# Where a query transpose starts, which buffer the extra keys leave through, and which of two transposes goes first

## The chip, the cores and the metric

The kernel runs on one core of one Trainium2 chip. The metric is the device time in microseconds (us) of one execution; lower is better. The core has a matrix engine (TensorE, PE in the profile), a vector engine (DVE), a scalar engine (ACT), GpSimd (POOL) and a queue engine (SP) that here does nothing but issue transfers. Each engine runs its own instruction stream in order, and engines wait for one another on semaphores.

## The reference

There are two parts. The first is a recurrent attention with memory over 2048 rows of width 640, in 64 segments of 32 rows, with 32 heads of width 128. The 8 memory rows of a segment are outputs of the segment before, so the segments follow one another strictly:

```
mem = mem0
for s in range(64):
    h = concat([mem, layernorm(x)[32*s : 32*s+32]])        # 8 + 32 rows
    q, k, v = h @ Wq, h @ Wk, h @ Wv                       # 640 -> 32 heads x 128
    p = softmax(where(mask, q @ k.T * scale, -1e9))        # memory rows see all, others causally
    o = (p @ v) @ Wo
    mem, out[s] = o[:8], o[8:]
h  = x + out
h2 = h + ((relu(layernorm(h) @ W_gate)) * (layernorm(h) @ W_up)) @ W_down
```

The second part, the last two lines, is a feed-forward block over all rows.

## The kernel before, in words

**The order is written by hand.** The function `add` records operations with the keys that they read and write; `solve` then derives the semaphore waits from these keys: an operation waits for the last writer of what it reads, and for all readers of what it overwrites. Each engine runs its operations in the order in which they were recorded. So a key in a list of reads is also a way to hold an operation back, and a buffer that a transfer still reads holds back whoever wants to fill it again.

**Steps.** The loop over `s` (L905) handles one segment per step. A step projects 32 rows through Wk, Wq and Wv: 8 memory rows, which are known only at the end of the step before, and 24 "rider" rows of later segments, whose normed values are known long in advance. A step therefore computes keys, queries and values that a later step needs. Since 24 riders per step are fewer than the 32 rows that a segment has, 32 more rows per four steps ("extra" rows, in `act_e`) are projected in gaps: in a step with s % 4 = 2 through Wk, with 3 through Wq, with 0 through Wv (`extra_units`, L858). The step with s % 4 = 1 fills the same gaps with the output projection of older rows (`woe_pass`). In what follows a step is called by its class, s % 4.

**Order inside a step.** TensorE: K projection (`project`, L422 and L400), Q projection, two fifths of V, `pick_mem` (L453, picks the memory queries), the rest of V, `scores` (L572), two gap pieces, `pv_mem` (L609), gap pieces, `trans_om` (L624), the last gap piece, `wo_pass` (L644, the new memory rows), `pv_x` (L690). Then the next step's K projection starts.

**Token buffers.** A projection leaves PSUM as rows (tokens) in `tok[0..3]`, copied by ACT and DVE (`to_tok`, which shows as L464 on ACT and L466 on DVE). K's rows go to `tok[0]` and `tok[1]`, which together are `tokp[0]`; Q's rows go to `tok[2]` and `tok[3]`, together `tokp[1]`. A DMA transpose from SP (`dma_t`, L363) turns `tokp[0]` into `KS`, and another, `trans_q`, turns `tokp[1]` into `QS`. From `KS`, DVE copies the riders' keys to the ring `Kr` (`evac_k`); from `QS`, ACT copies the riders' queries to the ring `Qr` (`evac_q`). `scores` of a step reads this step's own `KS` for the memory keys, and `Kr` and `Qr` as earlier steps left them. A third transpose per step, `trans_ox`, turns `ox` into `oT`.

**The place of `trans_q`.** In classes 0 and 1 (`qlate`) it stands at the end of the step and its copy goes into the next step through `late_k`. In classes 2 and 3 it stands early:

```
            qlate = nr and s % 4 < 2
            if nr and not qlate and s < NSEG - 2:
                trans_q()
            loads()
```

and its copy by ACT follows `exp_x` and `v_riders` in the same step.

**The extra keys** of class 2 are copied by ACT to `tok[2]` and `tok[3]` after the last gap piece and then transposed from `tokp[1]` straight to `Kr`. **The normed rows**: once per four steps, in class 2, DVE scales the rows `xt` of the next block (`row_scale`, L383), SP transposes them into `at`, and in the next step POOL copies them into the activations (`ln1_back`, L524). In four steps of class 0 (s = 32, 36, 40, 44) the same pair of operations handles rows of the feed-forward part. The transpose `at<-xt` is recorded after `pv_x`.

**Riders' values** go from `Vp` to the ring `Vr` by DMAs from POOL (`v_riders`, L501): eight in class 2, four in the others. Output rows leave by `attn_d<-wtok` and `attn_d<-at`, also from POOL.

**Probabilities of the memory queries**: `exp_mem` has ACT compute the exponentials into `om` (L582), and two DVE operations write them, masked, into `Pbd` (L585).

Of the kernel before, what the change touches and what calls it, by code (L numbers as in the profile page):

```python
# [208 lines left out]
def build_kernel(nc, A_x, A_mem0, A_Wq, A_Wk, A_Wv, A_Wo, A_seg_len, B_W_gate, B_W_up, B_W_down, out):  # L209
    _, S, D = A_x.shape  # L210
    M = A_mem0.shape[1]
# [4 lines left out]
    NSEG = S // SEG  # L216
# [145 lines left out]
    def dma_t(dst, src, r, w):  # L362
        add("sp", lambda e: e.dma_start_transpose(dst, src), r=r, w=w, dma=True)  # L363
# [65 lines left out]
    def to_tok(b, t, eng):  # L429
        copy_op(eng, tok[t][:, :], bank(b), [B(b)], [("tok", t)])  # L430
# [150 lines left out]
    def exp_mem():  # L581
        add("act", lambda a: a.activation(ap(om, 0, [[8, 2], [16, 8], [1, 8]]), s_view(0, M), ACTF.Exp,  # L582
                                          scale=SCALE), r=[B(P0), B(P1)], w=[("om",)])
        for i in range(2):
            add("dve", lambda v, i=i: v.tensor_tensor(ap(Pbd, 256 * i, [[32, 8], [16, 2], [1, 16]]),  # L585
                                                      ap(om, 0, [[16, 8], [0, 2], [1, 16]]),
                                                      ap(mbd, 32 * i, [[0, 8], [16, 2], [1, 16]]), ALU.min),
                r=[("om",), ("mbd",)], w=[("Pbd", i)])

    def exp_x():  # L590
        add("act", lambda a: a.activation(ap(Px, 0, [[32, 2], [64, 8], [1, 32]]), s_view(M, M + SEG),  # L591
# [266 lines left out]
    def extra_units(s):  # L858

        b, r = (s - 2) // 4, (s - 2) % 4
        t0 = 64 + 128 * b + 96
        if b < 0 or r == 3 or t0 >= S:
            return None, None, None
        a, ks = act_e[b % 2], [("acte", b % 2)]
        q = seg_slot(t0 // SEG)
        j = (1, 0, 2)[r]

        def part(n):
            project(a, ks, j, (0, 1), BQ, PARTS[n], j // 2)

        def evac():
            for i, e in enumerate(("act", "act")):
                if j == 2:
                    to_v(BQ[i], Vr[q], i, ("Vr", q), e)
                else:
                    to_tok(BQ[i], 2 + i, e)
            if j == 1:  # L880
                dma_t(Kr[q][:].rearrange("p h t -> p (h t)").rearrange("p (k r) -> p k r", r=128), tokp[1][:, :],
                      [("tok", 2), ("tok", 3)], [("Kr", q)])

        def fin():
            trans_q()
            late_q.append(lambda: evac_q(QS, ("QS",), t0, 32, 0, "act"))
        return part, evac, (fin if j == 0 else None)
# [17 lines left out]
    for s in range(NSEG):  # L905
        last = s == NSEG - 1
        q = seg_slot(s)
        nb = s // 4 + 1
        ln = 64 + 128 * nb < S

        e2 = EARLY.index(s // 4 * 4 + 3) if s // 4 * 4 + 3 in EARLY else None
        e2b = EARLY.index(s - 1) if s - 1 in EARLY else None
        def loads(s=s, e2=e2, e2b=e2b, nb=nb, ln=ln):
            if s % 4 == 3 and e2 is not None:
                dma(xt[:, :], x_ap[128 * e2:128 * e2 + 128, :], r=[("KS",)], w=[("xt",)])
                load_attn(at, e2, [], ("at",))
            if s % 4 == 0 and ln and e2b is None:
                ln1_load(nb, xt, ("xt",))
            if s % 4 == 1 and s - 2 in EARLY:
                e = EARLY.index(s - 2)  # L920
                dma(xn2_d[e], at[:, :], r=[("at",)], w=[("xn2_d", e)])
                if ln:
                    ln1_load(nb, xt, ("xt",))
        if s == 0:
            loads()
        if s > 0:
            a, ks, kn = pass_act(s)
            t0, nr = rider_tokens(s)
            project(a, ks, 1, (0, 1), BQ, (0, 1), spare=16)
            ks = ks + kn  # L930
            project(a, ks, 1, (0, 1), BQ, (2, 3, 4), spare=24)
            to_tok(BQ[0], 0, "act")
            to_tok(BQ[1], 1, "dve")
            if last:
                break
            dma_t(KS[:].rearrange("p h t -> p (h t)").rearrange("p (k r) -> p k r", r=128), tokp[0][:, :],
                  [("tok", 0), ("tok", 1)], [("KS",)])
            trans_ox()
            for f in late:
                f()  # L940
            late = []
            project(a, ks, 0, (0, 1), (P0, P1), spare=40)
            to_tok(P0, 2, "act")
            to_tok(P1, 3, "dve")
            for f in late_k + late_q:
                f()
            late_k, late_q = [], []
            qlate = nr and s % 4 < 2
            if nr and not qlate and s < NSEG - 2:
                trans_q()  # L950
            loads()
            project(a, ks, 2, (0, 1), (P2, P3), (0, 1), spare=16)
            if s == NSEG - 2:
                trans8(tok[2], ("tok", 2), tok[3], ("tok", 3), T0)
                copy_op("dve", Qr[:, :, q, 0:M], slots(T0, 0, M), [B(T0)], [("Qm", q)])
                evac_q(slots(T0, 0, SEG), B(T0), t0, nr, M, "act")
            else:
                pick_mem(T0)
                copy_op("dve", Qr[:, :, q, 0:M], bank(T0)[:, 0:256].rearrange("p (h t) -> p h t", t=M), [B(T0)], [("Qm", q)])
            if nr:  # L960
                evac_k(KS, ("KS",), t0, nr, M, "dve")
            project(a, ks, 2, (0, 1), (P2, P3), (2, 3, 4), spare=24)
            to_v(P3, Vp, 1, ("Vp", 3), "dve")
            to_v(P2, Vp, 0, ("Vp", 0), "act", 0, 2)
            scores(s)
            exp_mem()
            to_v(P2, Vp, 0, ("Vp", 1), "act", 2, 4)
            exp_x()
            if nr:
                v_riders(t0, nr)  # L970
                if s < NSEG - 2 and not qlate:
                    evac_q(QS, ("QS",), t0, nr, M, "act")
        units, evac, nfin = extra_units(s)
        woe = s % 4 == 1 and s >= 5

        def filler(n):
            if units:
                units(n)
            if woe:
                woe_pass(BQ[0], WPARTS[n])  # L980
        filler(0)
        filler(1)
        pv_mem(s)
        if s % 4 == 1 and s >= 5:
            copy_op("dve", oTn[:, :, :], oT[:, :, 0:M], [("oT", "m"), ("oT", "n")], [("oTn",)])
        elif s > 0:
            copy_oTe(s - 1)
        norm_om()
        filler(2)
        filler(3)  # L990
        trans_om(128 if s % 4 < 2 else 32)
        mask_x()
        n = n_rows(nb) if s % 4 == 2 and ln else 128 if e2b is not None else 0
        if n:
            row_scale(xt, ("xt",), n, xt, ("xt",))
        filler(4)
        if evac:
            evac()
        if woe:
            copy_op("dve", oTe[:, :, 0:M], oTn[:, :, :], [("oTn",)], [("oTe", 0)])  # L1000
            woe_sum(BQ[0])
            late.append(lambda b=s // 4 - 1: woe_store(b, [("KS",)]))
        if s == 0:
            wo_pass(T1, None, halves=(0,))
            keep_busy(P0)
            wo_pass(T1, None, halves=(1,))
        else:
            wo_pass(T1, MARKS[s % 4])
        if s == NSEG - 2:
            load_gate_up([("oTe", (s - 1) % 4), ("go", T1, 0)])  # L1010
        to_act(s + 1, B(T1), bank(T1)[:, 0:160])
        if s >= 1:
            wo_rows(T1, wtok[s % 2], ("wtok", s % 2), "act")
            store_attn(wtok[s % 2], ("wtok", s % 2), s - 1)
            if qlate and s < NSEG - 2:
                trans_q([("act", (s + 1) // 4 % 2, (s + 1) % 4, "m")])
                late_k.append(lambda t0=t0, nr=nr: evac_q(QS, ("QS",), t0, nr, M, "act"))
        pv_x(s, P0)
        if n:
            dma_t(chunks_of(at[:, :])[:, :, 0:n], xt[0:n, :], [("xt",)], [("at",)])  # L1020
            if s % 4 == 2:
                late.append(lambda nb=nb: ln1_back(nb, chunks_of(at[:, :]), [("at",)], "pool"))
        if nfin:
            nfin()
        norm_x(P0)
        if s % 4 == 1 and ln:
            late.append(lambda nb=nb: row_stats(xt, ("xt",), n_rows(nb)))
        if s % 4 == 3 and e2 is not None:
            def f(e2=e2):
                add_attn(xt[:, :], xt, at, [("xt",), ("at",)], [("xt",)])  # L1030
                dma(h_d[128 * e2:128 * e2 + 128, :], xt[:, :], r=[("xt",)], w=[("h_d", e2)])
                row_moments(xt, ("xt",), 128)
            late.append(f)
            late_q.append(lambda: row_rstd(128))
# [218 lines left out]
```

## Time and profile before

| what | value |
|---|---|
| three runs, median (lowest to highest) | 1100.82 us (1099.63 to 1101.9) |
| the profiled execution, its own time | 1100.57 us |
| its span, first to last instruction | 1098.8 us |
| time around the span | 1.8 us |
| TensorE busy in the span | 1057.8 us (96%) |
| DVE, ACT, POOL busy | 608.4, 362.6, 291.5 us |
| steps 2 to 62, mean length | 13.55 us |
| `QS`, `KS`, `oT` transposes | 76, 62, 62 |
| `Kr<-tok` and `at<-xt` transposes | 15 and 19 |

A line of the groups names the line of the code, the engine, the operation, what it writes and reads, and how often; after the bar come its busy time, the mean duration of one in ns, and the idle time of the engine before it with what ended it. In the view of DMA issues the last number is the median time in us from issue to landing. In a timeline the first column is the start in us from the start of the span, the second the length, and brackets hold the idle time before and what ended it; "SPq" is SP's queue, where a length is the time that issuing took, not the transfer.

A step is measured here from the first matmul of `pv_x` of the step before to that of its own, so times "in the step" count from there.

### The profile page before, as it was taken

How to read it: one execution, taken by the hardware profiler on the slowest of the kernel's cores; microseconds unless marked ns; L12 is line 12 of the kernel's file. 1: busy time of each engine (PE TensorE's matmuls, PEld its weight loads, DVE VectorE, ACT ScalarE, POOL GpSimd, SP SyncE). 2: the span in 40 equal slices, each digit the busy share in tenths (PEclk: the TensorE clock that was granted, in tenths of full speed). 3: DMA queues.
4: the chain of work that ended last, by engine and by line, in shares of the span. 5: the costliest groups of instructions: out<-in, count | busy, mean ns of one | idle time of the engine just before them, and what ended most of it. 6: DMA issues, size and time to landing. Idle time of an engine off the chain costs nothing.

```text
span 1098.8 us, 55766 instructions
## 1 busy us (share of the span) xinstructions
PE 1057.8 (96%) x27875; PEld 511.8 (47%) x23292; DVE 608.4 (55%) x1673; ACT 362.6 (33%) x792; POOL 291.5 (27%) x585
## 2 busy tenths in 40 slices
PE   4789999999999999999999999999999999999999
PEld 2454545444545444545444544444445455444444
DVE  3245656565656565666656665565656554553522
ACT  1213333333433433333333333333333332231211
POOL 1023233333333232323232323242323243000000
PEclk9989999999999999999999999999999999999999
DMA  9946464546464545556556556554455548132100
GB/s 360 387 91 113 87 108 88 104 90 104 91 101 90 103 90 100 94 109 111 112 104 112 108 112 107 101 97 93 94 101 93 92 96 313 43 80 72 31 18 24
DMA packets 285882, 121.60 MB, mean 111 GB/s; under 512 B 261392, under 2 KB 275300, under 8 KB 285648
## 3 DMA queue, kind: packets, MB, share of 16 engines
q1 hardware_dynamic: 265920, 93.92, 40.9%
q0 software_dynamic: 19312, 23.86, 9.6%
q8 instruction: 201, 3.29, 1.3%
q14 instruction: 33, 0.27, 0.1%
q10 hardware_dynamic: 416, 0.26, 0.1%
HBM read 36.79 MB, written 7.19 MB: 40 GB/s over the span
## 4 chain that ended last, share of the span: by engine, by line
PE 90%; DMA 5%; SPq 3%; DVE 1%; issue 1%; ACT 0%; DVEq 0%
PE ps L422 25%; PE ps L400 23%; PE ps L644 13%; PE ps L1051 11%; PE ps L666 3%; PE ps L690 3%; PE ps L572 3%; SPq L360 3%; PE ps L1092 3%; DMA Wo<-in_A_Wo_dram 3%; PE ps L609 2%; PE ps L453 2%; DMA QS<-tok 1%; DMA KS<-tok 1%; PE ps L624 1%
## 5 line engine op out<-in xcount | busy, mean ns | idle before, releaser
L422 PE MATMUL ps<-W,act_r 128*32 128x512 bf16 x4292 | 404.8, 385 | 6.5 <-DMA W<-in_A_Wv_dram 2.6
L400 PE MATMUL ps<-W,act_r 128*32 128x512 bf16 x3588 | 359.0, 379 | 0.0
L360 POOL DMA_DIRECT2D Vr<-Vp x376 | 187.2, 505 | 345.5 <-ACT Px L591 280.6
L422 PEld LDWEIGHTS ps<-W,act_r 128*32 128x32 bf16 x4292 | 126.0, 97 | 257.7 <-issue 157.2
L464 ACT ACTIVATE tok<-ps 128x512 bf16<-128x512 f32 x192 | 110.8, 593 | 228.4 <-PE ps L400 200.4
L644 PE MATMUL ps<-Wo,oT 128*32 128x160 bf16 x8064 | 156.9, 235 | 6.2 <-DMA Wo<-in_A_Wo_dram 3.1
L466 DVE CAST tok<-ps 128x512 bf16<-128x512 f32 x131 | 90.5, 691 | 130.1 <-PE ps L400 109.5
L644 PEld LDWEIGHTS ps<-Wo,oT 128*32 128x32 bf16 x8064 | 143.8, 98 | 26.6 <-DVE oT L466 16.8
L422 PE MATMUL ps<-W,act_e 128*32 128x512 bf16 x900 | 89.8, 381 | 0.0
L400 PE MATMUL ps<-W,act_e 128*32 128x512 bf16 x900 | 89.4, 379 | 0.0
L555 DVE STREAM_TRANSPOSE TBf<-ps 128x64 f32<-128x64 f32 (+1 forms) x128 | 33.6, 263 | 93.2 <-PE ps L644 93.2
L705 DVE TENSOR_TENSOR ox<-ps,rx 128x512 bf16<-128x512 f32 x128 | 82.5, 686 | 2.2
L464 ACT ACTIVATE Qr<-QS 128x512 bf16<-128x512 bf16 (+3 forms) x107 | 69.7, 680 | 38.4 <-DMA QS<-tok 38.4
L360 POOL DMA_DIRECT2D attn_d<-wtok x62 | 46.4, 748 | 130.8 <-ACT wtok L464 130.8
L464 ACT ACTIVATE Vp<-ps 128x256 bf16<-128x256 f32 (+1 forms) x126 | 48.5, 385 | 81.5 <-PE ps L400 79.0
L1066 DVE TENSOR_TENSOR hT<-g,ps 128x512 bf16<-128x512 bf16 (+1 forms) x56 | 38.5, 688 | 47.3 <-PE ps L1051 43.4
L1051 PE MATMUL ps<-xn2T,Wg 128*128 128x512 bf16 x260 | 64.6, 379 | 0.0
L1051 PE MATMUL ps<-xn2T,Wu 128*128 128x512 bf16 x260 | 64.6, 379 | 0.0
L1064 ACT ACTIVATE g<-ps 128x512 bf16<-128x512 f32 (+1 forms) x56 | 32.4, 592 | 91.6 <-PE ps L1051 91.6
L466 DVE CAST Vp<-ps 128x512 bf16<-128x512 f32 x64 | 44.2, 691 | 28.3 <-PE ps L400 22.3
L1092 PE MATMUL ps<-Wd,hT 128*128 128x320 bf16 x210 | 57.2, 299 | 0.0
L400 PE MATMUL ps<-Wd,hT 128*128 128x320 bf16 x210 | 57.2, 299 | 0.0
(121 smaller groups left out, 1151.8 us busy)
## 6 DMA issues: line engine op xcount, KB each, us to landing
Vr<-Vp POOLq DMA_DIRECT2D x124, 48.8 KB, 1.9
W<-in_A_Wk_dram SPq DMA_DIRECT2D x2, 2560.0 KB, 13.4
W<-in_A_Wq_dram SPq DMA_DIRECT2D x2, 2560.0 KB, 29.0
W<-in_A_Wv_dram SPq DMA_DIRECT2D x2, 2560.0 KB, 27.7
Wo<-in_A_Wo_dram SPq DMA_DIRECT2D x2, 2560.0 KB, 28.5
xt<-in_A_x_dram SPq DMA_DIRECT2D x30, 160.0 KB, 2.7
Vr<-Vp POOLq DMA_DIRECT2D x128, 32.5 KB, 2.3
at<-attn_d SPq DMA_DIRECT2D x16, 160.0 KB, 3.4
```

The costliest lines, as they stand in the source:

```text
L360: add(eng, lambda e: e.dma_start(dst, src), r=r, w=w, dma=True)
L400: return pe.add_instruction(mybir.InstMatmult(name=nc.get_next_instruction_name(), engine=mybir.EngineType.PE, ins=[pe.lower_ap(rhs), pe.l ...
L422: ins = pe.matmul(*a, start=(c == 0), stop=(c == DC - 1), skip_group_check=True)
L464: add("act", lambda a: a.activation(dst, src, ACTF.Copy), r=r, w=w)
L466: add("dve", lambda v: v.tensor_copy(dst, src), r=r, w=w)
L555: add("dve", lambda v, lo=lo, hi=hi: v.transpose(TBf[:, lo:hi, :].rearrange("p c t -> p (c t)"), src[:, 32 * lo:32 * hi]), r=[wkey], w=[(" ...
L572: i = pe.matmul(bank((P0, P1)[g % 2])[p:p + (M if a else 32), 40 * k:40 * k + 40], lh, Qr[:, h, q, :], start=True, stop=True, skip_group_c ...
L644: i = pe.matmul(bank(bk)[32 * gg:32 * gg + 32, 0:160], src[:, hb, :], w[:, gg], start=(hb == ORDER[0]), stop=(hb == ORDER[31]), skip_group ...
L705: add("dve", lambda v, kh=kh: v.tensor_tensor(ox[:, :, kh, :], src[:, :, kh, 0:128], ap(rx, kh, [[2, 4], [0, 128]]), ALU.mult), r=[B(b0 + ...
L1051: ins = pe.matmul(bank(bk), w[:, c, lo:lo + 128], xn2T[par][:, :, c, :], start=(c == 0), stop=(c == DC - 1))
L1066: add("dve", lambda v: v.tensor_tensor(hT[par][lo:128, j, :], g1[gi][lo:128, :], bank(bu)[lo:128, :], ALU.mult), r=[B(bu), ("g1", gi)], w= ...
L1092: i = pe.matmul(*a, start=(j == 0), stop=(j == FC - 1), skip_group_check=True)
```

## The change

There are four edits.

1. In class 2 (`qmid`) `trans_q` is no longer recorded early. It is recorded after `v_riders` and reads one more key, `("qgo", 1)`, which the second DVE operation of `exp_mem` now writes. The copies `QS` to `Qr` move from the end of that step to the next step, through `late_k`, behind that step's Q rows on ACT.
2. The extra keys of class 2 are copied to `tok[0]` and `tok[1]` and transposed to `Kr` from `tokp[0]`. The extra queries of class 3 still use `tok[2]` and `tok[3]`.
3. `at<-xt` is recorded right after `row_scale`, ahead of the last gap piece. On SP it now stands ahead of the `Kr` transpose in class 2, and ahead of `trans_q` in the four steps of class 0.
4. On TensorE the order stays the same. `scores` of class 3 carries one more wait, for the ACT copy of edit 1.

```diff
@@ exp_mem
-                r=[("om",), ("mbd",)], w=[("Pbd", i)])
+                r=[("om",), ("mbd",)], w=[("Pbd", i), ("qgo", i)])
@@ extra_units, evac
-                    to_tok(BQ[i], 2 + i, e)
+                    to_tok(BQ[i], 2 * (1 - j) + i, e)
             if j == 1:
-                dma_t(Kr[q][:].rearrange("p h t -> p (h t)").rearrange("p (k r) -> p k r", r=128), tokp[1][:, :],
-                      [("tok", 2), ("tok", 3)], [("Kr", q)])
+                dma_t(Kr[q][:].rearrange("p h t -> p (h t)").rearrange("p (k r) -> p k r", r=128), tokp[0][:, :],
+                      [("tok", 0), ("tok", 1)], [("Kr", q)])
@@ the loop over s
             qlate = nr and s % 4 < 2
-            if nr and not qlate and s < NSEG - 2:
+            qmid = nr and s % 4 == 2 and s < NSEG - 2
+            if nr and not qlate and not qmid and s < NSEG - 2:
                 trans_q()
...
                 v_riders(t0, nr)
-                if s < NSEG - 2 and not qlate:
+                if qmid:
+                    trans_q([("qgo", 1)])
+                if s < NSEG - 2 and not qlate and not qmid:
                     evac_q(QS, ("QS",), t0, nr, M, "act")
...
             row_scale(xt, ("xt",), n, xt, ("xt",))
+            dma_t(chunks_of(at[:, :])[:, :, 0:n], xt[0:n, :], [("xt",)], [("at",)])
         filler(4)
...
             store_attn(wtok[s % 2], ("wtok", s % 2), s - 1)
+            if qmid:
+                late_k.append(lambda t0=t0, nr=nr: evac_q(QS, ("QS",), t0, nr, M, "act"))
...
         if n:
-            dma_t(chunks_of(at[:, :])[:, :, 0:n], xt[0:n, :], [("xt",)], [("at",)])
             if s % 4 == 2:
```

## The prediction

> **What bounds the kernel now.** I read the page's busy times first: TensorE is busy for 96% of the span. Then what TensorE waited for, to see how much a change of order can win at all; then single steps in the table by stretches; then the timeline from step 14 (class 2) into step 15 (class 3), where the change acts; last the DMA issues.
>
> ```profile
> PE 1057.8 (96%) x27875; PEld 511.8 (47%) x23292; DVE 608.4 (55%) x1673; ACT 362.6 (33%) x792; POOL 291.5 (27%) x585
> ```
> ```profile
> PE ps L644 <- issue: 2.3, 7, 0.6
> PE ps L453 <- DVE tok L466: 1.9, 3, 1.0
> PE ps L572 <- DMA KS<-tok: 1.5, 3, 0.7
> ```
> ```profile
> 236.58:249.83 13.25, 13.23 (x423) 5.97 (x337) 8.99 (x26) 6.16 (x15) 5.68 (x12) 1.00 0.55 107
> 249.83:263.34 13.51, 13.49 (x421) 6.60 (x338) 7.56 (x21) 4.85 (x10) 4.57 (x11) 1.00 0.68 114
> ```
> ```profile
> 248.85 1.23 SPq L363 DMA_TRANSPOSE Kr<-tok  x1
> 250.19 1.73 SPq L363 DMA_TRANSPOSE at<-xt  x1
> 253.82 1.50 SPq L363 DMA_TRANSPOSE KS<-tok  x1
> ```
> ```profile
> 253.10 0.60 ACT L464 ACTIVATE tok<-ps 128x512 bf16<-128x512 f32 x1 [2.16 <-PE ps L400]
> ```
> ```profile
> QS<-tok SPq DMA_TRANSPOSE x76, 3.1
> KS<-tok SPq DMA_TRANSPOSE x62, 3.2
> at<-xt SPq DMA_TRANSPOSE x19, 4.9
> Kr<-tok SPq DMA_TRANSPOSE x15, 5.2
> ```
>
> Line 1 says that TensorE sets the time. The waits say that little idle time is booked in the loop: under 6 us in these three rows. The stretches (length, then busy time and count by engine) show a step at its floor, 13.25, and one 0.26 above it though TensorE counts as busy throughout, so a booked wait isn't the whole loss. Going through steps 2 to 61 in the timeline, the floors are 13.23 (class 0), 13.30 (1), 13.25 (2, 3), and the excess over them sums to some 1.9, 4.4, 6.7 and 5.6 us. About 18.6 us is thus all that the loop can win; only part of it lies where the change acts.
>
> The three SP rows and the ACT row carry the forecast. `Kr<-tok` is issued 12.27 us into step 14, and takes 4.9 us to land by the DMA view of that moment: 3.92 us into step 15. ACT fills `tok[0]` with K's rows at 3.27 there, 3.02 in an undelayed step. Today these two don't meet, since `Kr` reads `tok[2..3]`. The 12 landings of `Kr` that the trace holds lie 3.60 to 4.38 into class 3, mean 4.08.
>
> **What the Trainium skill says.** (1) "DMA: Bandwidth & Descriptors", section "Issuing engines are not separate DMA queues": transfers of all issuers share the same 16 engines and interleave. The trace agrees: `Kr`, which runs beside POOL's eight `Vr` transfers, needs 5.2 us where `QS` needs 3.1. (2) The same page, "Queues, rings and completion order": a completion is posted only after earlier writes of that DMA engine, across queues. That would explain the 5.2, but the trace doesn't separate it from plain sharing. (3) "Runtime: NRT & Kernel Launch", "Instruction fetch mechanics": a sequencer fetches blocks of 256 instructions, 16 KiB, over its own DMA queue. The trace has 201 instruction packets with 3.29 MB, 16.4 KB each; TensorE's small "issue" losses fall on the same matmuls of each class, as late blocks would.
>
> **The change part by part.**
>
> *Edit 1, 15 `QS` transposes and 30 ACT copies, class 2.* No instruction is added. On SP, `QS` leaves its place behind `oT` (issue at 6.7) for the time when `Pbd` is written, 9.26 (DVE writes it from 245.35 for 0.49, step from 236.58). Behind it on SP are only `at` and `Kr`, neither ready before 12.2, so the wait holds nothing up. It lands at about 12.4 by the 3.1 of the row above, or 15 if POOL's transfers slow it by what they cost `Kr`; needed by ACT at 5.2 of step 15, over 3 us later still. The copies (0.93 us a pair) go behind Q's rows on ACT, 5.8 to 6.7 in class 3, ahead of `scores` at 7.53: 0.8 us of cover, cost 0. If Q's rows were late by more, `scores` would wait. Class 3's own `trans_q` must now wait for these copies, 6.7; it is issued at 6.7 to 7.3 already, behind `oT`. Cost 0, up to 0.2 each off the path. Gain: in five class 2 steps (6, 30, 38, 50, 54) `wo_pass` stalls on issue, 0.36 three times and 0.09 twice; the instruction packet is seen at 10.2 there, against 9.2 elsewhere, while `QS` was on the rings. **-1.3 us**; bounds 0 and -1.3.
>
> *Edit 3, `at` first.* 19 transposes, none added. In class 2 `xt` is ready at 12.29, `Kr`'s rows at 12.20: `at` takes `Kr`'s slot and `Kr` moves back by one issue, 1.24 us, to 13.67, that is 0.42 into class 3. `at` also waits for POOL's stores of its old content, `attn_d<-at`, landed at 11.62 in step 14: 0.7 us of cover. The `at` transposes leave the stretch in which they collide with `KS` (landings at 6.2 to 7.3). The `scores` of class 3 that wait for `KS` lose 0.08 to 0.26 in seven steps: **-1.3 us**, which edit 2 must not use again. In the four class 0 steps `at` goes ahead of `QS`, and the next step has no `at` at 1.89 to 3.2: steps 33 and 45 lose 0.81 and 0.85 to a late `KS`, 37 and 41 together 1.8 on issue. I take the first two whole and half of the rest, **-2.6 us**; bounds 0 and -3.5. Issue losses in class 3's K projection, 1.75 us over seven steps, I leave, since `at` now runs where `Kr` ran; bounds -1.75 and +3.
>
> *Edit 2, the buffer.* This is the price. K's rows in class 3 may be written only when `Kr` has landed. ACT and DVE wait; queued behind them are Q's rows (5.2, unharmed as long as the wait ends before 4.5), on SP `KS` and `oT`, and on TensorE `scores`, which needs `KS`. Undisturbed, with rows at 3.02, `KS` lands at 6.78 (class 1 steps) and `scores` starts 0.14 after the landing wherever it waits (steps 3, 11, 47); TensorE gets there at 7.53. So 0.6 us of lateness is free and the rest is lost one for one: stall = landing of `Kr` + 0.05 - 3.62.
>
> The trace has no `Kr` behind an `at` in that window, so I bound it. Earliest: issue 0.42 plus 3.1, 3.5, stall 0. Latest: 0.42 plus 5.2, 5.6, stall 2.0. Between: `Kr` today, 4.08 though first in line; and the later one of the two transposes today, where `KS` did not queue behind it (steps 15, 31, 39, 51, 59): 4.58, 4.07, 5.00, 4.41, 4.63, mean 4.54, for the same total of bytes. I take the middle, 4.3: stall 0.72. Fifteen times: **+10.8 us**. Class 3's `oT` and `QS` follow later, and the `QS` transposes then run in the block fetch at 9.2; six such steps lose 2.6 us in `wo_pass` today. **+1.0**; bounds -2.6 and +4.
>
> *Sum.* -1.3 - 1.3 - 2.6 + 10.8 + 1.0 = +6.6. From the profiled execution's 1100.57 this makes 1107.2; the median shown is 0.25 above that execution, so 1107.4.
>
> **Rivals.**
>
> *A, faster.* With `QS` and `at` out of the way, `Kr` has quiet rings and lands as `QS` does, by 3.57. For it: `QS` issued at 0.61 lands at 3.68 to 3.75, and `Kr` issued at 0.53 in step 7 landed at 3.60. Against it: POOL's last `Vr` transfers land at 16.99 of step 14, and the moved `QS` makes them later. Edit 2 then costs nothing and the gains stay: -5.2, 1095.6.
>
> *B, no difference.* `Kr` lands at about 3.95, stall 0.38, 5.7 us, against -5.2: 1101.
>
> *C, much slower.* `QS` beside the `Vr` transfers pushes these into `at` and `Kr`; landing at 5.0, stall 1.43, 21.5 us; with 2 for fetches and less 5.2, +18.3, 1119.
>
> *D, the moved copy doesn't bite*: the `qgo` key could be met so early that `QS` runs where it did. It can't: in step 14 `Pbd` is complete at 9.26, and the old issue was at 6.69.
>
> What decides between the first three is one number: the forecast turns at a landing near 3.9.
>
> **How the numbers follow.** Main case (landing 4.0 to 4.7, 1103 to 1114) 0.50; A 0.25; B 0.12; C 0.13. A spans 1094 to 1098, C 1114 to 1122. About 0.1 below 1096 and 0.1 above 1116 is left out. A measurement can tell some 0.2%, 2.2 us, from no change. Faster is A, 0.25; same is B, 0.12; slower is the main case with C, 0.63. Within the slower cases alone the range is 1103 to 1118.
>
> **What would show it.** Right: in class 3, ACT's and DVE's first `tok` rows end their idle time on a `Kr` transfer; these rows start near 4.3 instead of 3.0; `scores` waits for `KS` in most of 15 steps; class 3 steps take about 14.2 us. Steps 33 and 45 fall to 13.3; `wo_pass` in class 2 is 2.33 everywhere. ACT's idle time before `Qr` copies, 38.4 us now, drops, which is worth nothing by itself. Wrong: `Kr` landing below 3.6 or the wait for the rows absent; class 2 steps longer, which would mean that the moved `QS` itself hurts.

## The result, and the profile after

The changed kernel takes **1140.42 us** (median of 4 runs, 1132.85 to 1146.65), the kernel before, in runs beside it, 1101.18 us. The ratio is 1.0355, interval 1.0273 to 1.0437: slower, by 39 us where 6.6 were foreseen. The profiled execution took 1134.77 us with a span of 1133.0, 34.2 above the span before; the 5.6 us between it and the median of its own runs are not explained by one trace.

From the page of after, the first part and the chain of work that ended last:

```profile
PE 1061.3 (94%) x27875; PEld 515.3 (45%) x23292; DVE 606.6 (54%) x1673; ACT 359.2 (32%) x792; POOL 290.4 (26%) x585
...
PE 78%; DMA 15%; SPq 3%; DVE 2%; issue 1%; ACT 0%; DVEq 0%
PE ps L422 20%; PE ps L400 19%; PE ps L644 13%; PE ps L1056 10%; DMA Kr<-tok 6%; DMA KS<-tok 4%; PE ps L666 3%; PE ps L572 3%; SPq L360 3%; DMA Wo<-in_A_Wo_dram 3%; PE ps L1097 3%; DMA QS<-tok 2%; PE ps L690 2%; PE ps L609 2%; PE ps L453 1%
```

TensorE does the same work, so its busy time grew by only 3.5 us; the rest of the 34 us is idle time. In the chain, transfers now hold 15% of the span, and `Kr<-tok` leads them with 6%. The waits of after say who stands behind that transfer (engine, line, waited for; total us, times, longest):

```profile
PE ps L453 <- DVE tok L466: 25.0, 18, 2.8
PE ps L572 <- DMA KS<-tok: 11.6, 14, 1.0
...
PE ps L644 <- issue: 0.2, 1, 0.2
```
```profile
ACT tok L464 <- DMA Kr<-tok: 76.6, 15, 6.3
```

`Kr` holds up ACT's copy of K's rows in all 15 class 3 steps. TensorE feels it in two places: `scores` (L572) waits for `KS`, as foreseen, and, at a higher cost, `pick_mem` (L453) waits for Q's rows, which stand behind K's rows on ACT and DVE. Of the two rows 11.2 and 18.4 us lie in class 3, each in 13 of its steps; in before the same views book none in class 3. (5.7 us of the L453 row belong to steps 33, 37, 41 and 45; the part on the prediction takes them up.) The wait at `pick_mem` is part of the same delay, since `scores` comes after it: in class 3 `scores` starts 10.26 us into the step on average instead of 7.74, so the whole loss of a step arises ahead of it.

The table by stretches shows step 14 (class 2) and step 15 (class 3) of after: length, then busy time and count of PE, PEld, DVE, ACT, POOL.

```profile
243.75:256.93 13.18, 13.18 (x420) 5.95 (x337) 8.98 (x26) 5.22 (x13) 5.77 (x12) 1.00 0.63 105
256.93:273.10 16.17, 13.93 (x421) 6.54 (x337) 7.46 (x21) 5.07 (x12) 4.48 (x11) 1.00 0.67 98
```

Step 14 is 0.07 us shorter than it was, step 15 is 2.66 longer. The timeline of SP's queue and of ACT from the end of step 14 (start, length):

```profile
255.95 1.20 SPq L363 DMA_TRANSPOSE at<-xt  x1
257.19 2.55 SPq L363 DMA_TRANSPOSE Kr<-tok  x1
263.99 1.23 SPq L363 DMA_TRANSPOSE KS<-tok  x1
```
```profile
263.27 1.09 ACT L464 ACTIVATE tok<-ps 128x512 bf16<-128x512 f32 x2 [5.23 <-DMA Kr<-tok]
```

`Kr` is issued 0.26 us into the step, and ACT can write K's rows only at 6.34; it then writes Q's rows at once ("x2"), since TensorE finished those long before. Over all class 3 steps of the trace `Kr` is issued at 0.94 on average and lands at 6.17 (mean of the 14 landings that the view of DMA issues has, 5.26 to 7.37).

The mean step by class (steps 2 to 61; "e2b" are the class 1 steps 33, 37, 41, 45, each behind one of the four class 0 steps that edit 3 changes) and the sum of the differences:

| class | before, us | after, us | sum over the steps, us |
|---|---|---|---|
| 0 | 13.36 | 13.27 | -1.4 |
| 1, without e2b | 13.33 | 13.31 | -0.2 |
| 1, e2b | 14.31 | 14.77 | +1.9 |
| 2 | 13.66 | 13.40 | -3.8 |
| 3 | 13.57 | 16.10 | +38.0 |

So the whole loss is in class 3.

### The profile page after: what moved, and what is told of

Same layout as the page of the kernel before. It is cut to its first block, busy times and chain, and to the rows that moved or that the text cites. A ratio compares the mean times of both kernels' runs of the same rounds, so it can differ in the third digit from the quotient of the medians.

```text
span 1133.0 us, 55766 instructions
## 1 busy us (share of the span) xinstructions
PE 1061.3 (94%) x27875; PEld 515.3 (45%) x23292; DVE 606.6 (54%) x1673; ACT 359.2 (32%) x792; POOL 290.4 (26%) x585
## 4 chain that ended last, share of the span: by engine, by line
PE 78%; DMA 15%; SPq 3%; DVE 2%; issue 1%; ACT 0%; DVEq 0%
PE ps L422 20%; PE ps L400 19%; PE ps L644 13%; PE ps L1056 10%; DMA Kr<-tok 6%; DMA KS<-tok 4%; PE ps L666 3%; PE ps L572 3%; SPq L360 3%; DMA Wo<-in_A_Wo_dram 3%; PE ps L1097 3%; DMA QS<-tok 2%; PE ps L690 2%; PE ps L609 2%; PE ps L453 1%
## 5 line engine op out<-in xcount | busy, mean ns | idle before, releaser
L422 PE MATMUL ps<-W,act_r 128*32 128x512 bf16 x4292 | 409.3, 387 | 7.6 <-DMA W<-in_A_Wv_dram 2.7
L400 PE MATMUL ps<-W,act_r 128*32 128x512 bf16 x3588 | 362.9, 381 | 0.0
L422 PEld LDWEIGHTS ps<-W,act_r 128*32 128x32 bf16 x4292 | 129.7, 98 | 258.1 <-issue 148.8
L466 DVE CAST Vp<-ps 128x512 bf16<-128x512 f32 x64 | 44.3, 692 | 25.6 <-PE ps L400 18.6
```

The costliest lines, as they stand in the source:

```text
L400: return pe.add_instruction(mybir.InstMatmult(name=nc.get_next_instruction_name(), engine=mybir.EngineType.PE, ins=[pe.lower_ap(rhs), pe.l ...
L422: ins = pe.matmul(*a, start=(c == 0), stop=(c == DC - 1), skip_group_check=True)
L466: add("dve", lambda v: v.tensor_copy(dst, src), r=r, w=w)
```

## The experiments

Each kernel was timed beside the kernel before; medians of before in these groups of runs were 1096.06 to 1098.75 us. "Edit 2 alone" means the kernel before with edit 2. Times "in the step" are in class 3.

### Is it the shared buffer? (own_all)

All four edits, but the extra keys leave through a buffer of their own, which shares its place with `oTn`:

```diff
-                    to_tok(BQ[i], 2 * (1 - j) + i, e)
+                    if j == 1:
+                        copy_op(e, tokx[:, 512 * i:512 * i + 512], bank(BQ[i]), [B(BQ[i])], [("tokx", i)])
+                    else:
+                        to_tok(BQ[i], 2 + i, e)
```

> All edits stay, but the extra keys leave through a buffer of their own (1024 elements per partition, which oTn shares), so K's rows in class 3 no longer wait for Kr. Theory 1 (the loss is K's rows waiting for the Kr transpose): class 3 steps fall from about 16.1 to 13.4 to 14.0 us and the time to 1097 to 1108. Rival (the moved transposes crowd the DMA rings, and KS itself comes late whatever buffer is used): class 3 stays above 15 us, the time above 1120.

Measured: 1100.64 us, ratio 1.0027 (1.0008 to 1.0046); class 3 takes 13.94. Its DMA issues, and ACT in the timeline of step 15 (which starts at 249.96):

```profile
Kr<-tokx SPq DMA_TRANSPOSE x15, 5.7
```
```profile
253.40 0.60 ACT L465 ACTIVATE tok<-ps 128x512 bf16<-128x512 f32 x1 [2.34 <-PE ps L401]
```

`Kr` is as slow as in after, 5.7 us from issue to landing, but nobody waits for it: ACT's idle time ends on TensorE, 3.44 into the step. This **shows** that the loss is K's rows waiting for `Kr`, and that a late `Kr` by itself costs little: class 3 keeps 0.37 us of the 2.53 that it had lost in a step.

### Which edits does it take? (k_buf, at_first, k_at, q_k)

Edit 2 alone (k_buf), edit 3 alone (at_first), edits 2 and 3 (k_at), edits 1 and 2 (q_k). Their diffs are the hunks of the change.

> Edit 2 alone: extra keys through tok[0..1], QS early and Kr ahead of at as before. Theory 1 with my model: Kr lands at 4.1 in class 3, stall 0.5 us in 15 steps, 1108. If edit 2 carries the whole loss by itself: above 1130. If Kr's lateness comes only from the moved QS: 1100 to 1110.

> Edit 3 alone: Kr lands late but reads tok[2..3], so only Q's rows could wait for it. Theory 1: Q's rows in class 3 are wanted at 5.2 and Kr lands at 5.8, so a stall of some 0.5 us at pick_mem in most of 15 steps, 1100 to 1110. If at first is harmless unless K's rows wait: 1096 to 1101. If at first costs by itself: above 1120.

> Edits 2 and 3, QS early as before. Theory 1: Kr, second behind at, lands at 4.3 to 4.6, stall 0.7 to 1.0, some 1112 to 1116. If edit 1 plays no part in the loss: 1130 to 1145.

> Edits 1 and 2, at behind pv_x as before. Theory 1 with the moved QS as the cause of Kr's lateness: Kr lands at about 5 in class 3, since at is not ahead of it, stall 1.4, 1115 to 1125. If at ahead of Kr is the main cause of the lateness: 1105 to 1110.

| edits | us | ratio (interval) | class 3, us | `Kr` issued, lands |
|---|---|---|---|---|
| 2 | 1108.7 | 1.0113 (1.0075 to 1.0152) | 13.68 | -0.78, 3.85 |
| 3 | 1113.05 | 1.0141 (1.0098 to 1.0183) | 14.28 | 0.31, 5.90 |
| 2 and 3 | 1134.56 | 1.0351 (1.0295 to 1.0407) | 15.74 | 0.63, 5.81 |
| 1 and 2 | 1110.51 | 1.0115 (1.0078 to 1.0152) | 14.54 | -1.04, 4.61 |
| 1, 2 and 3 (after) | 1140.42 | 1.0355 (1.0273 to 1.0437) | 16.10 | 0.94, 6.17 |

Edit 1 changes nothing in the sum that these intervals could show: 1.0113 against 1.0115, and 1.0351 against 1.0355. It does move time: with edit 2 it takes class 2 from 13.94 to 13.40 us, and class 3 from 13.68 to 14.54, with `Kr` landing 0.76 later. Edits 2 and 3 cost 10 and 15 us alone and 36 together. Edit 3 alone hurts although K's rows are on time (3.27): there `Kr` leaves through `tok[2..3]`, and Q's rows wait for it. The waits of at_first:

```profile
PE ps L453 <- DVE tok L466: 17.6, 17, 1.9
```

Of these 17.6 us, 11.4 lie in class 3 and 4.1 in steps 37, 41 and 45. So whichever token buffer the extra keys use, a landing near 6 is too late for it; K's buffer is only the worse one, since Q's rows queue behind K's.

### Is a late issue enough? (k_hold, own_q, own_q_hold)

k_hold is edit 2 alone with `Kr` held until the new memory rows are written, which brings its issue to 0.61, as late as in k_at:

```diff
-                      [("tok", 0), ("tok", 1)], [("Kr", q)])
+                    [("tok", 0), ("tok", 1), ("act", (s + 1) // 4 % 2, (s + 1) % 4, "m")], [("Kr", q)]))
```

> Edit 2 alone, with the Kr transpose held back until the new memory rows are written, some 0.6 us into class 3, at still behind it. So Kr is issued as late as under edit 3, but without at in front. If the late issue is what made Kr land at 5.8: landing near 5.8 again, 1125 to 1135. If it is at's data in front of it: landing 3.6 to 3.9, K's rows at 3.7 to 4.0, 1102 to 1109.

Measured: 1103.46 us, ratio 1.0047 (1.0018 to 1.0076). Issued 1.4 us **later** than in k_buf, `Kr` lands **earlier**, at 3.69 to 3.76 in every step. Its DMA issues, and its queue and ACT in step 15 (from 250.90):

```profile
Kr<-tok SPq DMA_TRANSPOSE x15, 3.1
```
```profile
251.51 1.23 SPq L363 DMA_TRANSPOSE Kr<-tok  x1
252.83 1.24 SPq L363 DMA_TRANSPOSE at<-xt  x1
...
254.69 0.60 ACT L464 ACTIVATE tok<-ps 128x512 bf16<-128x512 f32 x1 [2.69 <-DMA Kr<-tok]
```

3.1 us from issue to landing, where k_buf has 4.9 and after 5.3 in the same view, and issued in 1.23 us, where step 15 of after took 2.55. So it is not lateness that makes `Kr` slow, but what is going on when it runs. own_q is edit 1 with the separate buffer and `at` behind; own_q_hold adds the hold.

> Edit 1, and edit 2 with a buffer of its own for the extra keys instead of tok[0..1]; at behind pv_x as before. Theory 1: nothing waits for Kr, class 2 keeps its gain of 0.25 us a step, 1095 to 1100. Rival: the moved QS slows KS in class 3: 1103 or more.

> The kernel with edit 1 and a buffer of its own for the extra keys, with Kr held back until the new memory rows are written, so that it starts on quiet rings. If held transposes finish sooner for all behind them: class 3 steps 13.3 to 13.5, 1092 to 1096. If at behind it then collides with KS: 1097 to 1102.

Measured: own_q 1096.45 us, ratio 0.9987 (0.9969 to 1.0005), the fastest of all and not to be told from before; own_q_hold 1099.34, 1.0008 (0.9989 to 1.0028). Without the shared buffer the hold has nothing to save. (own_q_hold has the moved `QS` too. There the held `Kr` lands by 3.77 in nine of 15 steps and at 4.71 to 6.37 in the other six; the part on the instruction fetch comes back to them.)

### What slows Kr: bytes, POOL's transfers, a second transpose? (k_at_split, k_at_norid, k_alone)

```diff
@@ k_at_split: edits 2 and 3, one of at's five chunks ahead of Kr, four behind pv_x
-            dma_t(chunks_of(at[:, :])[:, :, 0:n], xt[0:n, :], [("xt",)], [("at",)])
+            dma_t(chunks_of(at[:, :])[:, 0:1, 0:n], xt[0:n, 0:128], [("xt",)], [("at",), ("at4",)])
...
+            dma_t(chunks_of(at[:, :])[:, 1:5, 0:n], xt[0:n, 128:640], [("xt",)], [("at4",)])
@@ k_at_norid: edits 2 and 3, class 2's Vr transfers left out
-                v_riders(t0, nr)
+                if not (s % 4 == 2 and s < NSEG - 2):
+                    v_riders(t0, nr)
@@ k_alone: edit 2, class 2's at recorded in the next step, behind KS and oT
+            def at_t(n=n):
+                dma_t(chunks_of(at[:, :])[:, :, 0:n], xt[0:n, :], [("xt",)], [("at",)])
+            if s % 4 == 2:
+                late.append(at_t)
```

> Edits 2 and 3, but only one of at's five 128-column chunks goes ahead of Kr; the other four follow it. Kr is issued one transpose later, as under edit 3. If at's bytes ahead of Kr push it into the crowded stretch and onto the block fetch: landing 4.0 to 4.9, class 3 steps 13.9 to 14.8 us, 1106 to 1120. If any transpose ahead of it is enough: landing 5.5 to 6, 1130 or more.

> Edits 2 and 3, without the eight Vr transfers that POOL issues in class 2 (the riders' values of those steps are left out). If these transfers slow the transposes beside them: at lands near 2.0 and Kr at 3.7 to 4.5, 1103 to 1115. If transposes stall one another whatever POOL does: Kr at 5.5 or more, above 1128.

> Edit 2 alone, and the class 2 transpose at<-xt moved out of Kr's way: it is issued in the next step, behind KS and oT. Kr then has no other SP transpose beside it, ahead or behind; POOL's Vr transfers stay. Theory (a second transpose in the rings is what makes Kr late, in this place too): Kr, issued near -0.8, lands by 2.5 to 3.2 instead of 3.85, K's rows don't wait (start near 3.0 to 3.3), class 3 near 13.5 to 13.7, ratio 0.998 to 1.004. Rival (the standing still of all transposes between 0.4 and 2.4 us into the step is what counts, with or without a second transpose): landing 3.6 to 3.9 as with edit 2 alone, ratio 1.008 to 1.013. Second rival (the at transpose beside KS and oT delays these instead): Kr lands early but TensorE waits for KS or Q's rows in class 3 or 0, ratio over 1.005 with K's rows on time.

k_at_split missed the first of its two expectations: 1136.37 us, 1.0345 (1.03 to 1.039), landing 6.43. With a fifth of the bytes ahead `Kr` is no earlier. k_at_norid fell between its two: 1134.13 us, 1.0308 (1.026 to 1.0356), landing 5.07 in the mean. Without POOL's `Vr` transfers `Kr` still lands at 5.4 to 6.9 in eight of 15 steps, but at 3.8 to 4.4 in the other seven, where k_at has one so early. So these transfers (rival C's cause) have a share in how often `Kr` is late, but it is late without them too, and the time is that of k_at. k_alone missed its theory: with no other transpose beside it `Kr` lands at 3.85, exactly as in edit 2 alone. (Its 1116.12 us, 1.0182 (1.0149 to 1.0215), come from class 0, 14.27 instead of 13.36: `at` behind `oT` now makes class 3's `QS` late, and in nine of 15 class 0 steps ACT's Q rows wait for it.) So a second transpose in flight isn't the cause of the 5 us either, at the place where before and k_buf have it.

### The instruction fetch (k_at_shift, k_buf_early, k_buf_late, k_at_early)

The packets in the trace gave the next theory. TensorE's sequencer fetches its instructions in blocks of 16,384 bytes (queue q8 moved 201 of them). In class 3 there are two such fetches, each of about 1.1 us: in k_at the first runs from about -0.2 to 1.1 in the step, the second from about 4.2 to 5.4. In k_buf the 256-byte packets of the transposes come nearly to a standstill in 11 of 15 class 3 steps, from 60 to 110 in 0.1 us down to about 4; in each of them they go on 0.6 to 1.4 us, in seven of them 0.8, after the end of the **first** fetch. (In three of the 11, steps 23, 35 and 43, they slow down only after that fetch has ended, so not every standstill is so plainly tied to it.) The four `Kr` that were issued at 0.27 or later don't stand. In after and k_at, landings fall 1.03 to 1.22 us after the end of the **second** fetch in 13 of the 28 that were seen (5 in after, 8 in k_at). `MARKS` sets where in `wo_pass` a block begins. k_at_shift (edits 2 and 3) moved it early in class 2, with extra weight loads to make up for it:

```diff
-    MARKS = (160, 108, 124, 140)
+    MARKS = (157, 108, 61, 231)
```

> Edits 2 and 3 with TensorE's 256-instruction blocks shifted by up to 98 doubled weight loads a step, so that the block fetch of class 3 starts at about 2 us into the step instead of 3.7 to 4.8. If Kr's completion sits behind that fetch: Kr lands at 4.4 to 5.0, the time falls from 1134 to 1112 to 1124. If Kr's data alone are late: Kr at 5.5 or later, 1128 or more.

Missed both ways: 1164.6 us, 1.0591 (1.0548 to 1.0634), landing 5.69. The first fetch did come 0.7 us earlier and the standstill was gone in at least 8 of 15 steps, but the second fetch then began at 3.1 to 4.2, in 8 of 15 within 0.03 us of `Kr`'s last data packet, and 12 of 14 landings came 1.03 to 1.6 us after its end. (The time says little here, since the added weight loads and the other moved blocks cost TensorE time of their own: at `pv_x` alone it waits 15.6 us for instructions.) The other three kernels move all blocks by some 60 instructions without more of them in the loop: k_buf_early and k_at_early earlier, with `(160, 108, 61, 140)`, k_buf_late later, with `(60, 168, 184, 200)`.

> Edit 2 alone, with every TensorE instruction-block boundary 60 instructions earlier (some 0.55 us in wo_pass), without more instructions in the loop. Theory (a block fetch holds the transposes that are in flight until 0.8 us after its end): the fetch at the step's start runs at about -0.8 to 0.4 instead of -0.2 to 1.0, Kr's packets go on by 1.2 instead of 1.8, and Kr lands near 3.2 to 3.5 instead of 3.85; class 3 about 13.5, if nothing else stalls. Rival (the standstill belongs to the transposes themselves or to POOL's Vr transfers, the fetch only happens to be there): landing unchanged, 3.7 to 4.0. The ratio says little, since the fetches of all classes move.

> Edit 2 alone, with every block boundary 60 instructions later. Theory: fetch at 0.4 to 1.6, Kr's packets stand still until 2.4, landing 4.3 to 4.8 (more where the next fetch overtakes its completion, then 1.0 to 1.2 us after that fetch's end); class 3 0.5 to 1 us longer than with edit 2 alone. Rival: landing unchanged, 3.7 to 4.0.

> Edits 2 and 3, with every block boundary 60 instructions earlier. Theory: the fetch at the step's start ends near 0.4, at and Kr go on by 1.2, Kr's data are out by 3.4 to 3.8; where the next fetch starts before that (it should come near 3.3 to 4), Kr still lands 1.0 to 1.2 us after its end, so 5.3 to 5.9, in the others near 4. Mean landing 4.6 to 5.7, below the 5.81 of edits 2 and 3. Rival: unchanged, 5.6 to 6.0, with no tie to the fetch's end.

The times are 1152.8 us (1.0494, 1.0444 to 1.0544), 1185.66 us (1.0773, 1.0712 to 1.0834) and 1176.02 us (1.0695, 1.0653 to 1.0736), since the fetches of every class move; the landings are what was asked for. From the packets of k_buf_late, us in the step:

```
step   first fetch    packets go on   after its end   Kr lands
  3    1.33 - 2.26        3.08            0.82           4.25
 11    1.53 - 2.51        3.35            0.84           4.01
 19    0.92 - 1.88        2.72            0.84           3.81
 31    0.38 - 1.62        2.43            0.81           4.63
 47    1.67 - 2.83        3.65            0.82           4.56
 59    1.50 - 2.60        3.44            0.84           4.63
```

The end of the standstill follows the end of the fetch, 0.8 us behind, wherever the fetch was put: in all 11 steps where `Kr` was issued ahead of it. There `Kr` lands at 4.34 in the mean, within what was expected, against 4.03 in the 11 steps of k_buf that have a standstill. In the other four steps it was issued at 0.86 to 1.73, met the next fetch, and landed 0.98 to 1.13 us after its end, at 6.2 to 7.8. Earlier blocks (k_buf_early) left a standstill in 1 step of 15; nine `Kr` landed at 3.15 to 3.37 as foreseen, but the mean of all 15 is 3.54, just above the expected 3.2 to 3.5, in part because the next fetch reached some `Kr` before they were complete (two landed 1.0 us after its end, at 4.29 and 4.89). Its issue had also moved, from -0.78 to -0.01, as class 2 grew; k_buf_late is the clean one of the pair. k_at_early has a mean of 5.70, at the upper edge of what was expected, with 10 of 15 landings 1.05 to 1.3 us after the second fetch, and one at 3.85, ahead of it.

So the standstill is **shown** to be the fetch's: it moved with it. own_q_hold agrees: the six `Kr` that land at 4.71 to 6.37 are those whose first fetch ends at 1.53 or later; in the nine others, by 3.77, it ends by 1.39. That a late `Kr` lands one microsecond after the second fetch is seen in after, k_at, k_at_shift, k_at_early and k_buf_late, but no run moved this fetch by itself, so here the tie is observed, not shown.

The trace holds two more details. A transpose reports its completion in sixteen semaphore updates. In the landings that follow the second fetch in after, k_at and k_at_shift, it is one of the sixteen that is late: in step 35 of after fifteen come at 5.06 to 5.23 and the last at 6.76. The last is over 0.6 us behind the other fifteen in 5 of 15 steps of after, 9 of k_at and 13 of k_at_shift, and in none of k_buf, k_hold or k_alone. And the standstill isn't complete: from the end of the fetch until the others go on, some 25 packets go out, mostly no more than two at a time. Both would fit one DMA engine that carried the fetch and has its own share to make up while the rest wait, but the packets in the trace bear no engine's number, so this stays a guess. If it is so, the late completion follows from the Trainium skill, "DMA: Bandwidth & Descriptors", section "Queues, rings and completion order" (a completion is posted only after earlier writes of that DMA engine, across queues). Why the data packets of all the other engines wait for a fetch stays open.

What the other kernels did to TensorE by the same means, in the waits of k_buf_early and of k_buf_late:

```profile
PE ps L690 <- issue: 34.3, 30, 1.8
```
```profile
PE ps L609 <- issue: 39.9, 31, 2.3
```

TensorE goes on 1.2 to 1.8 us after the end of a block fetch in each of these 61 waits, so it had run out of instructions: 34 us at `pv_x`, 40 at `pv_mem`, where the kernel before loses 2.3 in its largest such row. Why these fetches come so late is not shown. The transposes aren't always the reason: in k_buf_early none of their packets moves in the 1.6 us ahead of any of the 30 fetches.

## Why the prediction was right or wrong, point by point

**The bound and the path: right.** TensorE sets the time, the change acts through class 3, and the link `Kr` to K's rows to `KS` to `scores` is the one that broke.

**The step that failed is the landing of `Kr` in edit 2: 4.3 was taken, 6.17 measured**, beyond even the upper bound of 5.6. It is made of two misses. The issue: 0.42 was taken, with 1.24 us for issuing `at`; while the packets stand still issuing stretches, `at` took 1.84 on average, and `Kr` was issued at 0.94. The transit: 3.9 us was taken, 5.2 measured. The bounds were built from transfers of before as if a duration belonged to a transfer; it belongs to the time at which it runs. The trace of before already held this: its ten `Kr` that were issued ahead of 0 met the first fetch and took 4.5 to 5.7 us, the five that were issued at 0.20 to 0.60 took 3.1 to 4.0, and all those landings, 3.60 to 4.38, came before the second fetch ended. In after `Kr` stands behind `at`, which is itself held up by the first fetch, and in all 15 steps the second fetch begins before `Kr` has landed. Fifteen of the sixteen completions are in at 5.53 on average, which is already close to the upper bound; the last comes at 6.13 (all 15 steps). In five steps this last one is 1.4 to 1.6 us behind the others, 1.03 to 1.08 after the end of the second fetch: there the landing jumps instead of sliding. The prediction named these fetches as a likely cause of TensorE's small losses, and did not ask what they do to transfers. It also read the 5.2 of `Kr` against the 3.1 of `QS` as the cost of sharing the DMA engines with the `Vr` transfers; but k_at_norid, without them, still has 5.0 where k_at has 5.4, so the 5.2 was no evidence of that.

**The formula held.** Stall = landing + 0.05 - 3.62 gives 2.60 for after, where class 3 grew by 2.53; 2.24 for edits 2 and 3, where it grew by 2.17; 1.04 for edits 1 and 2, where it grew by 0.97. (For edit 2 alone it gives 0.28, and class 3 grew by 0.11, which is 1.7 of its 10 us; in its trace class 2 grew by 4.3 us, and this is not explained.) One link was missing: Q's rows "unharmed as long as the wait ends before 4.5". It ends at 6.2, and `pick_mem` became the larger wait.

**A reading that was off without harm.** With the floors that are given, the excess of the steps comes to 1.9, 4.3, 6.1 and 4.7 us, some 17 in all; nothing rests on the 18.6.

**Edit 1, gain 1.3, cost 0: the gain came, the cost was missed.** `wo_pass` in class 2 is 2.33 throughout but for two steps at 2.42, and class 2 fell by 3.8 us, of which `wo_pass` accounts for 1.1. The gain is there in every trace: 13.34 to 13.45 us for class 2 in the five kernels with edit 1, 13.66 to 13.94 in the eight without it whose blocks are in place. But the moved `QS` makes `Kr` later, by 0.36 us on top of edits 2 and 3 and 0.76 on top of edit 2, and with the shared buffer class 3 pays for that. own_q has edit 1 without the sharing, and there the whole kernel is 1.5 us below before, which its interval can't tell from no change.

**Edit 3, the 1.3 of late `KS`: overtaken** by edit 2, which made `KS` later than it had been.

**Edit 3, -2.6 in steps 33 and 45 and their like: wrong in sign.** These four steps sum to +1.9. They scatter, and the trace of before had them long: against it the six other kernels without edit 3 (blocks in place) sum to -2.5 to -0.9, the six with it to -1.3 to +3.2, so edit 3 costs some 2 us here in the mean (an estimate from these sums) and gains nothing. The working counted what `KS` gains once `at` is gone from 1.9 to 3.2, but not what `QS` loses behind `at`. In step 33 `QS` was issued at 0.61 and landed at 3.73; now it is issued at 1.30 and lands at 6.80, and Q's rows start at 6.88 instead of 5.18; `pick_mem` waits for them in all four steps, 5.7 us in sum. From the timeline of ACT in before (step 33 starts at 492.55) and in after (510.03):

```profile
497.72 0.60 ACT L464 ACTIVATE tok<-ps 128x512 bf16<-128x512 f32 x1 [1.56 <-PE ps L400]
```
```profile
516.91 0.60 ACT L464 ACTIVATE tok<-ps 128x512 bf16<-128x512 f32 x1 [3.26 <-DMA QS<-tok]
```

**The +1.0 for fetches in class 3's `wo_pass`: about +0.6.** By the length of `wo_pass`, which is how the prediction read its 2.6 us, class 3 exceeds 2.33 by 2.6 us in sum in before and by 3.3 in after. The row of booked waits, 0.2 us, shows almost nothing of it.

**The rivals.** A (quiet rings, `Kr` by 3.57): k_hold shows that such rings exist, 3.72, but not where the change puts `Kr`. B falls with it. C had the right direction, but the `Vr` transfers are not the main cause: without them the time stayed at 1134. D is out, as argued: the moved `QS` is issued when `Pbd` is written, 9.13 us into step 14.

**The signs listed under "what would show it"**: K's rows ending their idle time on `Kr` in all 15 steps and `scores` waiting for `KS` in 13 of them came true (the 14th such wait is in step 42, class 2); "near 4.3" and "about 14.2 us" became 6.2 and 16.1.

## What to carry to other kernels

A buffer that a slow transfer still reads must not be the one that the next stage fills first: a buffer of its own for the extra keys took away 36 of the 39 us. Before a transfer's duration from a profile is used at another place, look at the packets around it: if its packets stand still or its completion comes just after an instruction fetch, the duration is that of the place: `Kr` was issued 1.5 us later than in before and landed 2.1 later. And two edits that each cost little can push the same transfer across such an edge, so price them together.

## What the runs showed of the hardware that was not expected

- Transposes between tiles in SBUF nearly stand still while one of TensorE's instruction blocks of 16,384 bytes is fetched (about 1.1 us), until some 0.8 us after its end. Take the stretches of 0.4 us or more, with transposes in flight, in which no more than six of their packets start in 0.1 us but at least 20 in all: 26 of 27 in k_buf_late, 32 of 32 in k_at_shift and 14 of 14 in before end 0.6 to 0.9 us after a fetch. The Trainium skill, "Runtime: NRT & Kernel Launch", section "Instruction fetch mechanics", calls the cost of crossing a block "mostly hidden". For TensorE in the kernel before that holds, with 2.3 us in the largest row; in k_buf_early, with 34.3, it does not, and for the transfers beside it neither: 5.3 us for `Kr` in after, 3.1 in k_hold.
- A transpose that is not complete when the fetch begins can land 1.0 to 1.2 us after the fetch's end, as 11 of 14 do in k_at_shift, and then it is one of its sixteen completions that is late.
- Issued later, a transfer can land earlier: -0.78 led to 3.85, 0.61 to 3.72.
- Moving all block boundaries by some 60 instructions, with the same work, costs 44 us one way and 77 the other (k_buf_early and k_buf_late against k_buf).
